# Token-major linear attention with routing inside it, feeding a top-1 mixture of experts: five row tiles per expert and a left-over loop

## The chip, the cores and the metric

The kernel runs on one core of a Trainium2 chip. The metric is the device time of one execution in microseconds (us); the kernel before has a median of 692.61 us over three runs. The engines are TensorE (PE, with its weight loads PEld), VectorE (DVE), ScalarE (ACT), GpSimd (POOL) and the queue engine SyncE (SP). DMAs are issued from the SP queue and from POOL's.

## What is computed

```python
kv  = np.einsum('bhsd,bhse->bhde', k, v)          # q, k, v: 8 x 8 heads x 576 x 64, f32
out = np.einsum('bhsd,bhde->bhse', q, kv)
rms = np.sqrt(np.mean(out * out, axis=-1, keepdims=True) + 1e-06)
x   = (out / rms * g_norm) -> rows of 8 heads * 64 = 512, N = 4608 tokens
logits = x @ w_gate                               # 512 x 8
expert_idx = argmax(logits); gate_w = softmax(logits)[expert_idx]
for e in range(8):                                # w1: 512 x 1024, w2: 1024 x 512
    out[mask_e] = gate_w[mask_e] * (relu(x[mask_e] @ w1[e]) @ w2[e])
```

With the inputs of this kernel the eight experts get 564, 494, 600, 572, 539, 654, 585 and 600 tokens.

## The kernel before

The work stands in three stages, one after the other.

**Attention** (L131 to L215) runs over 8 batches and 4 pairs of heads. It works feature-major: q is turned by PE transposes (`qtp`, L151) and copied by DVE (`qts`, L157), k and v give `kvf` (L161, five f32 matmuls of 128x128 for a pair of heads, of which only the two diagonal 64x64 blocks are copied out), and `otp` (L174, L175) is 128 features by 576 tokens. ACT squares it, a matmul with `sel` (L182) sums the squares over the features, ACT takes Ln and Exp (L185, L187), and DVE multiplies into `roll` (L189) and casts into `xp01`/`xp23` (L198). The logits of each 128 tokens are four f32 matmuls with 8 moving columns (`lgp`, L207). q, k and v come in 256-byte runs on the SP queue (L136 to L142), with two buffers for a batch's `qkv`.

**Routing** (L222 to L325): x is turned back to token rows (L226, L232) and written to the scratch `x16d` (L233); the logits of all tokens give positions by a prefix sum on DVE, and 36 rounds of three DVE operations and one matmul (L299 to L311) turn positions into a list of tokens per slot (`ipv`, `ipu`) and the sorted gates.

**Experts** (L354 to L405): every expert has a capacity `CAP` of 1024 slots, 8 tiles of 128, filled or not. For each expert POOL issues two weight loads that cast to f16 (L349, L351), 8 gathers of rows (L338) and 8 scatters of results (L397). PE does 32 transposes (`xet`, L365), 64 matmuls `hp` of 512 columns (L377) and 64 matmuls `yp` (L390); ACT applies relu (L384), and DVE scales by the gate into `ysb` (L396, 3 buffers). Each scatter writes to the whole of `out`, so it waits for the scatter before it to land.

The order on each engine is set by the framework's scheduler, not by the order in which the code is written; waits between engines, on reused buffers and on overlapping DRAM writes are put in by the framework.

## Time and profile before

| | us |
|---|---|
| median of 3 runs | 692.61 (690.14 to 693.09) |
| span of the profiled execution | 691.4 |
| attention, from the first matmul to the last logits | 10 to 302 |
| routing tables and the scratch of x | 302 to 344 |
| first weights and gathers, start of the first expert | 344 to 374 |
| experts | 374 to 680 |
| last scatters and the end | 680 to 691.4 |

The median lies 1.2 us above the span. In the page, the clock line (PEclk) gives TensorE's granted clock in tenths of full speed, so 1.00 in a window is 2.4 GHz and 0.50 is 1.2 GHz; the DMA line is the busy share of the 16 DMA engines. A line of the trace with f32 matmuls counts two instructions for one matmul of the program, except for transposes, which count one.

### The profile page before, as it was taken

What the parts mean: (1) busy time and instruction counts of PE and PEld (TensorE: products, weight loads), DVE (VectorE), ACT (ScalarE), POOL (GpSimd) and SP (SyncE); (2) the same over time, 40 slices, a digit from 0 to 9 for tenths busy, and PEclk for the clock granted to TensorE, in tenths of its full rate; (3) what the DMA queues carried; (4) which work ended last, traced back from release to release, by engine and by line L of the source; (5) the groups of instructions that cost most, each with busy time, mean ns of one, the idle gap of its engine ahead of it and who ended that gap; (6) DMA issues with size and microseconds to landing.
All of it is one profiled execution on the core that took longest, in us unless ns stands there. A gap on an engine that the chain in (4) does not pass through costs nothing. (4 is left out here: it accounts for less than half of the span.)

```text
span 691.4 us, 6499 instructions
## 1 busy us (share of the span) xinstructions
PE 525.5 (76%) x2458; PEld 321.5 (46%) x2458; DVE 228.1 (33%) x569; ACT 145.6 (21%) x226; POOL 139.4 (20%) x148
## 2 busy tenths in 40 slices
PE   2688787879797879677809569698887959699890
PEld 1547575747474747465604234243433424244440
DVE  0142625252525252569901131212213121222220
ACT  0021313141313131300005005050321305031310
POOL 0000000000000000000055436162544526222222
PEclk9999957586657675757858979998999999999996
DMA  8969191928282900013289726455554626541010
GB/s 144 209 100 182 37 169 35 171 49 157 49 158 51 154 0 1 0 67 134 76 174 186 140 64 128 104 111 118 118 106 100 124 77 119 110 93 46 25 46 26
DMA packets 140302, 68.40 MB, mean 99 GB/s; under 512 B 118639, under 2 KB 131823, under 8 KB 140272
## 3 DMA queue, kind: packets, MB, share of 16 engines
q1 hardware_dynamic: 119536, 33.38, 26.1%
q0 software_dynamic: 20736, 34.63, 24.4%
q8 instruction: 19, 0.31, 0.2%
q14 instruction: 11, 0.09, 0.0%
HBM read 70.59 MB, written 21.50 MB: 133 GB/s over the span
## 5 line engine op out<-in xcount | busy, mean ns | idle before, releaser
L390 PE MATMUL yp<-w2e,hT 128*128 128x512 f16 x512 | 125.0, 402 | 41.5 <-DVE ysb L396 41.4
L384 ACT ACTIVATE hT<-hp 128x512 f16<-128x512 f32 x128 | 76.4, 597 | 278.6 <-PE hp L377 278.6
L396 DVE TENSOR_SCALAR ysb<-yp,gsort 128x512 f32<-128x512 f32 x64 | 48.0, 751 | 239.1 <-DMA out_dram<-ysb,ipu 108.2
L377 PE MATMUL hp<-xsE,w1e 128*128 128x512 f16 x512 | 117.5, 386 | 0.0
L390 PEld LDWEIGHTS <-hT 128*128 128x128 f16 x512 | 52.1, 102 | 112.6 <-issue 59.7
L397 POOL DMA_INDIRECT out_dram<-ysb,ipu x64 | 63.2, 987 | 174.8 <-DMA out_dram<-ysb,ipu 75.3
L161 PE MATMUL kvf<-qkv 128*128 128x128 f32 (+1 forms) x320 | 72.8, 389 | 9.1 <-DMA qkv<-in_v_dram 9.1
L349 POOL DMA_DIRECT2D w1e<-in_moe_w_dram x8 | 7.0, 870 | 346.8 <-DVE ipv L324 346.8
L377 PEld LDWEIGHTS <-w1e 128*128 128x128 f16 x512 | 50.3, 99 | 56.8 <-issue 1.8
L207 PE MATMUL lgp<-wgt,roll 128*128 128x8 f32 x288 | 62.0, 342 | 12.9 <-DVE roll L189 12.9
L161 PEld LDWEIGHTS kvf<-qkv 128*128 128x128 f32 (+1 forms) x320 | 61.3, 277 | 16.5 <-issue 9.2
L207 PEld LDWEIGHTS lgp<-wgt,roll 128*128 128x128 f32 x288 | 60.2, 307 | 16.8 <-DVE roll L189 16.2
L338 POOL DMA_INDIRECT xe<-x_scratch,ipv x64 | 61.5, 961 | 26.5 <-issue 11.9
L180 ACT ACTIVATE sq<-ots 128x576 f16<-128x576 f32 x32 | 21.8, 682 | 196.4 <-DVE ots L177 196.4
L174 PE MATMUL otp<-qts,kv 128*128 128x512 f32 x64 | 50.9, 888 | 12.8 <-DVE qts L157 10.9
L365 PE MATMUL xet<-ident,xe 128*128 128x128 f16 x256 | 25.2, 236 | 28.8 <-issue 16.1
L157 DVE COPY qts<-qtp 128x576 f32<-128x576 f32 x32 | 24.2, 758 | 68.5 <-PE qtp L151 68.2
L151 PE MATMUL qtp<-ident,qkv 128*128 128x128 f32 (+1 forms) x160 | 37.0, 349 | 9.8 <-DMA qkv<-in_q_dram 9.8
L365 PEld LDWEIGHTS <-xe 128*128 128x128 f16 x256 | 19.7, 106 | 39.3 <-issue 34.8
L182 PE MATMUL msp<-sq,sel 128*128 128x512 f16 x32 | 15.4, 483 | 25.6 <-ACT sq L180 24.0
L151 PEld LDWEIGHTS qtp<-ident,qkv 128*128 128x128 f32 (+1 forms) x160 | 23.9, 178 | 23.0 <-issue 20.4
L189 DVE SCALAR_TENSOR_TENSOR roll<-ots,g,rst 128x576 f32<-128x576 f32 x32 | 26.1, 816 | 23.4 <-ACT rst L187 22.5
(61 smaller groups left out, 325.0 us busy)
## 6 DMA issues: line engine op xcount, KB each, us to landing
qkv<-in_q_dram SPq DMA_DIRECT2D x32, 256.0 KB, 4.9
qkv<-in_k_dram SPq DMA_DIRECT2D x32, 256.0 KB, 5.1
qkv<-in_v_dram SPq DMA_DIRECT2D x32, 256.0 KB, 5.2
w1e<-in_moe_w_dram POOLq DMA_DIRECT2D x8, 1024.0 KB, 8.7
w2e<-in_moe_w_dram POOLq DMA_DIRECT2D x8, 1024.0 KB, 9.2
x_scratch<-xtk SPq DMA_DIRECT2D x36, 128.0 KB, 1.7
qkv<-in_q_dram SPq DMA_DIRECT2D x8, 128.0 KB, 5.0
qkv<-in_k_dram SPq DMA_DIRECT2D x8, 128.0 KB, 4.5
```

The source lines that it names most:

```text
L151: nc.tensor.transpose(qtp[:, c * 128 : c * 128 + L], qkv[:L, c, 0, h0 : h0 + 2, :], ident[:L, :L],)
L161: nc.tensor.matmul(kvf, qkv[:L, c, 1, h0 : h0 + 2, :], qkv[:L, c, 2, h0 : h0 + 2, :], start=(c == 0), stop=(c == 4),)
L174: nc.tensor.matmul(otp[:, 0:512], kv2, qts[:, 0:512], start=True, stop=True)
L189: nc.vector.scalar_tensor_tensor(out=roll[:, i, rcol : rcol + 576], in0=ots, scalar=g2, in1=rst, op0=ALU.mult, op1=ALU.mult,)
L207: nc.tensor.matmul(lgp, roll[:, i, lc : lc + 128], wgt[:, i, :], start=(i == 0), stop=(i == 3),)
L338: nc.gpsimd.indirect_dma_start(out=xe, out_offset=None, in_=x16d.ap(), in_offset=IndirectOffsetOnAxis(ap=ipv[:, g : g + 1], axis=0),)
L365: nc.tensor.transpose(xet[:, cset, :], xcur[gg][:, cset * 128 : (cset + 1) * 128], ident16,)
L377: nc.tensor.matmul(hp, w1e[:, kk, f * 128 : (f + 1) * 128], xsE[:, kk, ws * 512 : ws * 512 + 512], start=(kk == 0), stop=(kk == 3),)
L384: nc.scalar.activation(hT[:, f, ws * 512 : ws * 512 + 512], hp, ACTF.Relu)
L390: nc.tensor.matmul(yp, hT[:, ft, cg * 128 : (cg + 1) * 128], w2e[:, ft, :], start=(ft == 0), stop=(ft == 7),)
L396: nc.vector.tensor_scalar(ysb, yp, gsort[:, g : g + 1], None, op0=ALU.mult)
L397: nc.gpsimd.indirect_dma_start(out=out, out_offset=IndirectOffsetOnAxis(ap=ipu[:, g : g + 1], axis=0), in_=ysb, in_offset=None, bounds_che ...
```

## The change

The kernel is written anew. Attention is token-major: `x_tile` handles 128 tokens at a time for all 8 heads (36 tiles), with the turned q stationary and `kvs` moving. `kvs` has 144 columns for a pair of heads: the 128 of kv, and 16 with kv times the gate weights (`kgp`), so the logits fall out of the same matmul. The sums over features are a DVE reduction along the row. `kv_stage` computes only the 64x64 blocks. g_norm moves into `gw` and into w1, which POOL now multiplies and casts after a plain f32 load.

`route` runs after every 4 or 5 tiles: it ranks the tokens within their expert by matmuls with triangular and all-ones matrices, puts token number and gate into the last 4 halfwords of each row, and POOL scatters the rows of 1032 bytes straight to `xs`, which has room for all tokens in each expert. `dram_disjoint_views` tells the framework that the scatters into `xs` and into `out` don't overlap. The weights of six experts are loaded during attention into six buffers.

Each expert has 5 tiles of 128 slots (CAP 640); `left_over` handles what is above, one tile always and more in a loop whose count comes from the data. With these inputs only expert 5 is over 640, by 14 tokens, so the one tile is used and the loop is not entered.

```diff
-    CAP = 1024
+    CT = 5
+    CAP = CT * 128
...
+    xs_views = dram_disjoint_views(xs.ap(), N // 128)
+    out_views = dram_disjoint_views(out, E * CT + 2)
...
+    def load_w(e, stage):
+        e = e if isinstance(e, bass.DynSlice) else slice(e, e + 1)
+        w1e = P_w.tile([128, 4, F], F16, tag="w1e", bufs=6, name="w1e")
+        w2e = P_w.tile([128, 8, D], F16, tag="w2e", bufs=6, name="w2e")
+        for kk in range(4):
+            st = stage.tile([128, F], F32, tag="wst", bufs=2, name="wst")
+            nc.gpsimd.dma_start(
+                st, moe_w1[e, kk * 128:(kk + 1) * 128, :].rearrange("o p f -> p (o f)")
+            )
+            nc.gpsimd.tensor_scalar(
+                w1e[:, kk, :], st, g2, 1.0, op0=ALU.mult, op1=ALU.mult
+            )
+        nc.gpsimd.dma_start(
+            w2e, moe_w2[e, :, :].rearrange("o (t p) d -> p (o t) d", p=128)
+        )
+        return w1e, w2e
...
+        def load_qkv(src, b, tag, bufs):
...
+            nc.sync.dma_start(
+                t, src[b, :, 0:512, :].rearrange("h (p j) d -> p h (j d)", j=4)
+            )
...
+        def load_q(b):
...
+            for j in range(4):
+                nc.sync.dma_start(t[:, j, :, :], qv[:, :, j, :])
...
+        def kv_stage(b, kb, vb, kr, vr):
...
+            for i in range(4):
+                for j in range(5):
+                    for hh in range(2):
...
+                        if j < 4:
+                            lhs = kb[:, h, 64 * j:64 * j + 64]
...
+                        nc.tensor.matmul(
+                            kvp[64 * hh:64 * hh + 64, i, :], lhs, rhs,
+                            start=(j == 0), stop=(j == 4),
+                        )
...
+            for hh in range(2):
+                ps = slice(64 * hh, 64 * hh + 64)
+                nc.vector.tensor_copy(kvs[ps, :, 64 * hh:64 * hh + 64], kvp[ps, :, :])
+            kvtp = PSA.tile([128, 4, 128], F32, tag="misc", bufs=1, name="kvtp")
+            for i in range(4):
+                nc.tensor.transpose(kvtp[:, i, :], kvs[:, i, 0:128], ident)
+            kvt = PA.tile([128, 4, 128], F32, tag="kvt", bufs=1, name="kvt")
+            nc.scalar.copy(kvt, kvtp)
...
+            for i in range(4):
+                nc.tensor.matmul(
+                    kgp[:, i, :], kvt[:, i, :], gw[:, i, :, :], start=True, stop=True
+                )
+            nc.vector.tensor_copy(kvs[:, :, 128:144], kgp)
+            return kvs
+        def x_tile(qsrc, parts, xg, lr, t):
...
+            for i in range(4):
+                nc.tensor.transpose(qtp[:, i, :], qsrc(i), ident)
+            qts = PA.tile([128, 4, 128], F32, tag="qts", bufs=2, name="qts")
+            nc.scalar.copy(qts, qtp)
+            op = PSA.tile([128, 2, 512], F32, tag="op", bufs=2, name="op")
+            for i in range(4):
+                c0 = (i % 2) * 144
+                for c, kvs in parts:
+                    nc.tensor.matmul(
+                        op[c, i // 2, c0:c0 + 144],
+                        qts[:, i, c],
+                        kvs[:, i, :],
+                        start=True,
+                        stop=True,
                     )
...
+            nc.scalar.activation(
+                sq.rearrange("p (c i h) n -> p c i (h n)", c=2, i=2),
+                oc[:, :, :, 0:128], ACTF.Square,
+            )
...
+            nc.vector.reduce_sum(ms, sq, axis=AXX)
...
+            nc.scalar.activation(lnt, ms, ACTF.Ln, scale=1.0 / 64.0, bias=epsb)
...
+            nc.scalar.activation(rinv, lnt, ACTF.Exp, scale=-0.5)
...
+            nc.vector.tensor_tensor(
+                xg[:, t, 0:512].rearrange("p (c i h n) -> p c i h n", c=2, i=2, h=2),
+                ox,
+                _bc(r4, 4, 64),
+                op=ALU.mult,
+            )
+            nc.vector.tensor_tensor(
+                lr[:, t, :, :].rearrange("p (c i h) n -> p c i h n", c=2, i=2),
+                ol,
+                _bc(r4, 4, 8),
+                op=ALU.mult,
+            )
...
+        def route(G, xg, lr, tile0):
...
+            nc.tensor.matmul(pp, ones, _bc(cs16, 1, G), start=True, stop=False)
+            for t in range(G - 1):
+                nc.tensor.matmul(
+                    pp[:, t + 1:G, :], ones, _bc(oh[:, t, :], 1, G - 1 - t),
+                    start=False, stop=False,
+                )
+            nc.tensor.matmul(pp, utri, oh, start=False, stop=True)
...
+            for t in range(G):
+                nc.gpsimd.indirect_dma_start(
+                    out=xs_views[tile0 + t],
+                    out_offset=IndirectOffsetOnAxis(ap=sli[:, t:t + 1], axis=0),
+                    in_=xg[:, t, :].bitcast(I32),
+                    in_offset=None,
+                )
+        for P in range(4):
...
+            kb = load_qkv(k, b0, "kb", 1)
+            vb = load_qkv(v, b0, "vb", 1)
...
+            qb0 = load_q(b0)
+            qr = load_rem(q, b0, "qr", 2)
+            kvs0 = kv_stage(b0, kb, vb, kr, vr)
...
+            for j in range(4):
+                x_tile(
+                    lambda i: qb0[:, j, 2 * i:2 * i + 2, :],
+                    [(slice(0, 128), kvs0)], xg, lr, j,
+                )
...
+            route(4, xg, lr, 9 * P)
+            kvs1 = kv_stage(b0 + 1, kb, vb, kr, vr)
+            if P < 3:
+                weights[2 * P] = load_w(2 * P, P_w)
...
+        def ffn(xe, nt, w, okm, bgm, views):
...
+            cols = nt * 128
+            halves = 2 if cols > 512 else 1
+            wd = cols // halves
...
+            for ws in range(halves):
+                for f in range(8):
...
+                nc.gpsimd.indirect_dma_start(
+                    out=views[t],
+                    out_offset=IndirectOffsetOnAxis(ap=idx[:, t:t + 1], axis=0),
...
+        def left_over(t, t0, view):
...
+            w = load_w(bass.ds(ev, 1), P_w)
...
+            ffn([gather(xe_bufs[t0], gi)], 1, w, okm, bgm, [view])
...
+        xcur = load_x(0)
+        for e in range(E):
+            xnext = load_x(e + 1) if e + 1 < E else None
+            if e + 6 < E:
+                weights[e + 6] = load_w(e + 6, P_w)
+            ffn(xcur, CT, weights[e], valid[:, e, :], bigm[:, e, :],
+                out_views[e * CT:(e + 1) * CT])
+            xcur = xnext
+        left_over(0, 2 * CT, out_views[E * CT])
+        nov = nc.values_load(tabi[0:1, 1, 7:8], min_val=0, max_val=NOV)
+        with tc.If(nov > 1):
+            with tc.For_i(1, nov) as t:
+                left_over(t, 2 * CT + 1, out_views[E * CT + 1])
```

Three places show what the scheduler makes of it. The first is PE inside attention. Before, in the middle of a batch (`otp` is the product with kv, `msp` the sum of squares, `lgp` the logits):

```order
L174 MATMUL otp<-qts,kv_339 128x512
L175 MATMUL otp<-qts,kv_339 128x64
L207 MATMUL lgp<-wgt,roll 128x8
L182 LDWEIGHTS sel
L182 MATMUL msp<-sq,sel 128x512
L183 LDWEIGHTS sel
L183 MATMUL msp<-sq,sel 128x64
L151 MATMUL qtp<-ident,qkv 128x128 x4
L151 MATMUL qtp<-ident,qkv 128x64
```

Now, at the end of the third pair's first batch (`op` is the product with kv and the logits, `pp` the ranks in `route`, `kvp` the next batch's kv):

```order
L218 MATMUL op<-kvs_94,qts 128x144 x8
L211 MATMUL qtp<-cf,qb 128x128 x8
L285 LDWEIGHTS ch
L285 MATMUL pp<-cs_1233,ch 128x32
L218 MATMUL op<-kvs_94,qts 128x144 x8
L287 LDWEIGHTS ch
L287 MATMUL pp<-oh,ch 128x24
...
L291 LDWEIGHTS ch
L291 MATMUL pp<-oh,ch 128x32
L186 MATMUL kvp<-vb,kb 64x64 x8
```

The rank matmuls, which need the result of the last two tiles (`oh`), stand in PE's queue ahead of the next batch's `kvp`. The second place is POOL's queue. Before, it holds nothing but a branch ahead of the first weight load and the gathers behind it:

```order
L349 DMA w1e_2113<-in_moe_w_dram 128x4x1024 [waits DMAHW3_49,DMAHW2_49,DMAHW4_49,DMAHW1_49,DMAHW5_49,DMAHW0_49,DMAHW6_49,DVE_49,DMAHW7_49,PE_49,Activation_49]
L351 DMA w2e_2115<-in_moe_w_dram 128x8x512
L338 DMA xe_2117<-x_scratch,ipv 128x512
L338 DMA xe_2119<-x_scratch,ipv 128x512
L338 DMA xe_2121<-x_scratch,ipv 128x512
```

Now it holds during attention (here the end of the first pair's first batch and the beginning of its second):

```order
L131 TENSOR_SCALAR w1e<-wst,g_65 128x1024 [waits DMASW4_49]
L131 TENSOR_SCALAR w1e<-wst,g_65 128x1024 [waits DMASW5_49]
L304 DMA xs_scratch<-xg,sli 36864x258 [waits DVE_49]
L304 DMA xs_scratch<-xg,sli 36864x258 x2
L304 DMA xs_scratch<-xg,sli 36864x258 [waits DMASW2_49]
L128 DMA wst<-in_moe_w_dram 128x1024 [waits DMASW3_49,Pool_49]
L128 DMA wst<-in_moe_w_dram 128x1024 [waits Pool_49]
L134 DMA w2e<-in_moe_w_dram 128x8x512
```

Weight loads and casts now stand between the row scatters in one queue: 10 of the 24 w1 pieces and all six w2 loads are issued ahead of the second batch's scatters. The third place is POOL in the experts' stage. Before, in expert 0:

```order
L397 DMA out_dram<-ysb,ipu 4608x512 [waits DMASW5_49,DVE_49]
L397 DMA out_dram<-ysb,ipu 4608x512 [waits DMASW6_49,DMASW5_49,DVE_49]
L397 DMA out_dram<-ysb,ipu 4608x512 [waits DMASW7_49,DMASW6_49,DVE_49]
L397 DMA out_dram<-ysb,ipu 4608x512 [waits DMASW7_49,DMASW0_49,DVE_49]
L397 DMA out_dram<-ysb,ipu 4608x512 [waits DMASW1_49,DMASW0_49,DVE_49]
```

Now, in a late expert:

```order
L476 DMA out_dram<-ys,idx 4608x512 [waits DMASW6_49,DVE_49]
L502 DMA xe_82<-xs_scratch,rowi 128x258 [waits DMASW7_49,PE_49]
L476 DMA out_dram<-ys,idx 4608x512 [waits DMASW0_49,DVE_49]
L502 DMA xe_83<-xs_scratch,rowi 128x258 [waits DMASW1_49,PE_49]
L476 DMA out_dram<-ys,idx 4608x512 [waits DMASW2_49,DVE_49]
```

Before, a scatter waits for the semaphore of the scatter just ahead of it (DMASW5, then 6, 7, 0); now it waits only for the semaphore that was used eight POOL DMAs earlier and for its data.

## Rows read from the trace of the kernel before

**Rows 1.** The page: span, granted clock and DMA share in 40 slices.
```profile
span 691.4 us, 6499 instructions
...
PEclk9999957586657675757858979998999999999996
DMA  8969191928282900013289726455554626541010
```
**Rows 2.** Stretches: start:end, length, busy of PE, PEld, DVE, ACT, POOL, PEclk, DMA share, GB/s.
```profile
10.00:302.00 292.00, 231.49 (x960) 175.06 (x959) 113.86 (x258) 67.42 (x96) 0.00 (x0) 0.74 0.56 96
302.00:344.00 42.00, 32.74 (x213) 24.29 (x214) 40.33 (x172) 0.44 (x1) 0.00 (x0) 0.74 0.32 113
344.00:374.00 30.00, 13.44 (x73) 7.95 (x73) 5.03 (x19) 4.46 (x8) 18.16 (x19) 0.61 0.92 162
374.00:680.00 306.00, 247.65 (x1215) 114.00 (x1213) 68.22 (x120) 71.98 (x121) 118.09 (x122) 0.94 0.46 98
```
**Rows 3.** Waits, by total: engine and line, whom for: us, times, longest.
```profile
POOL w1e L349 <- DVE ipv L324: 346.8, 1, 346.8
...
DVE ysb L396 <- DMA out_dram<-ysb,ipu: 108.2, 36, 11.9
...
PE yp L390 <- DVE ysb L396: 41.4, 16, 10.0
```
**Rows 4.** Timeline of PE in attention: start us, us, engine, line, operation, count.
```profile
12.22 1.20 PE L161 MATMUL kvf<-qkv 128*128 128x128 f32 x4 [1.97 <-DMA qkv<-in_v_dram]
...
62.14 4.50 PE L161 MATMUL kvf<-qkv 128*128 128x128 f32 x18
...
72.06 0.84 PE L151 MATMUL qtp<-ident,qkv 128*128 128x128 f32 x5
...
79.67 0.56 PE L207 MATMUL lgp<-wgt,roll 128*128 128x8 f32 x4
...
89.82 6.14 PE L207 MATMUL lgp<-wgt,roll 128*128 128x8 f32 x28 [1.49 <-DVE roll L189]
...
102.43 2.39 PE L161 MATMUL kvf<-qkv 128*128 128x128 f32 x16
...
115.79 1.39 PE L151 MATMUL qtp<-ident,qkv 128*128 128x128 f32 x5
```
**Rows 5.** Groups by line: shapes, count | busy us, mean ns | idle before.
```profile
L189 DVE SCALAR_TENSOR_TENSOR roll<-ots,g,rst 128x576 f32<-128x576 f32 x32 | 26.1, 816 | 23.4 <-ACT rst L187 22.5
...
L157 DVE COPY qts<-qtp 128x576 f32<-128x576 f32 x32 | 24.2, 758 | 68.5 <-PE qtp L151 68.2
...
L180 ACT ACTIVATE sq<-ots 128x576 f16<-128x576 f32 x32 | 21.8, 682 | 196.4 <-DVE ots L177 196.4
...
L274 DVE SCALAR_TENSOR_TENSOR pos<-ix,ss 128x36 f32<-128x36 f32 x1 | 0.2, 196 | 0.0
```
**Rows 6.** Two stretches by the columns of rows 2: early attention, one expert.
```profile
20.00:60.00 40.00, 31.21 (x103) 21.75 (x102) 13.86 (x31) 8.44 (x12) 0.00 (x0) 1.00 1.06 163
...
411.00:448.00 37.00, 31.96 (x159) 14.53 (x157) 7.62 (x14) 9.56 (x16) 16.76 (x18) 0.95 0.56 116
```
**Rows 7.** POOL's indirect DMAs: a group by line, and issues with us to landing.
```profile
L338 POOL DMA_INDIRECT xe<-x_scratch,ipv x64 | 61.5, 961 | 26.5 <-issue 11.9 <-DMA w2e<-in_moe_w_dram 7.4 <-PE hp L377 5.8
...
xe<-x_scratch,ipv POOLq DMA_INDIRECT x64, 4.4
out_dram<-ysb,ipu POOLq DMA_INDIRECT x64, 2.7
```
**Rows 8.** Timeline of the experts' stage, by the columns of rows 4.
```profile
447.61 0.61 PE L365 MATMUL xet<-ident,xe 128*128 128x128 f16 x8
...
452.75 12.90 PE L377 MATMUL hp<-xsE,w1e 128*128 128x512 f16 x59
...
659.84 12.25 PE L390 MATMUL yp<-w2e,hT 128*128 128x512 f16 x56
...
687.66 0.97 POOL L397 DMA_INDIRECT out_dram<-ysb,ipu  x1 [1.87 <-DMA out_dram<-ysb,ipu]
```

More of the change, by code (lines that the diff above doesn't have):

```diff
@@ L127 @@
+    weights = {}
     with (
@@ L202 @@
-            while (next_w + 1) * 128 <= (b + 1) * 576:
-                w = next_w
-                lc = 128 * (w % 9)
-                lgp = PSA.tile([128, 8], F32, tag="KV", bufs=2)
-                for i in range(4):
-                    nc.tensor.matmul(
-                        lgp,
-                        roll[:, i, lc : lc + 128],
-                        wgt[:, i, :],
-                        start=(i == 0),
-                        stop=(i == 3),
-                    )
-                nc.vector.tensor_copy(logits[:, w, :], lgp)
-                next_w += 1
@@ new lines @@
+        cs16 = PA.tile([128, 8], F16, tag="cs16", bufs=2, name="cs16")
+        nc.vector.tensor_copy(cs16, csum)
+        cp = PSA.tile([128, 8], F32, tag="misc", bufs=1, name="cp")
+        nc.tensor.matmul(cp, ones, cs16, start=True, stop=True)
+        cnt = PA.tile([128, 8], F32, tag="cnt")
+        nc.vector.tensor_copy(cnt, cp)
+        nc.vector.tensor_tensor(valid, _bc(rankc, 1, E), _bc(cnt, 2, CT), op=ALU.is_lt)
+        nc.vector.tensor_scalar(
+            bigm, valid, -BIG, BIG, op0=ALU.mult, op1=ALU.add
+        )
@@ new lines, in gather, with load_x @@
+        def gather(xe, rows):
+            nc.gpsimd.indirect_dma_start(
+                out=xe.bitcast(I32),
+                out_offset=None,
+                in_=xs.ap(),
+                in_offset=IndirectOffsetOnAxis(ap=rows, axis=0),
+                bounds_check=E * N - 1,
+                oob_is_err=False,
+            )
+            return xe
+        def load_x(e):
+            return [
+                gather(xe_bufs[(e % 2) * CT + t], rowi[:, e, t:t + 1])
+                for t in range(CT)
+            ]
```

511 lines of the change are left out of this document (240 added, 271 removed).

## The prediction

> **What bounds the kernel now.** I read the page's slices first, then the stretches, then the waits, and only then single rows. The slices show a clock near half speed and a DMA share that comes in bursts up to slice 16, a DMA pause, and a clock near full speed from slice 23 [rows 1]. The stretches say where the 691.4 us go: 292 us of attention with PE busy for 231 of them at a mean granted clock of 0.74, 42 us in which DVE is busy for 40.3 (routing), 30 us in which PE does 13 us of work and the DMA share is 0.92, and 306 us of experts with PE busy for 248 at 0.94 [rows 2]. So PE bounds attention and the experts, DVE the routing, and the first loads the start of the experts. The waits show what is loose: POOL issues no weight load before 346.8 us, since that waits for the routing; and in the experts PE waits 41.4 us for DVE, which waits 108.2 us for the previous scatters to land [rows 3]. The sum below is made against the span; the median is 1.2 us above it.
>
> **Attention, 292 us to some 252.** The prices on PE first, for a matmul of the program (two lines in f32, one for a transpose). A 128x128 kv matmul takes 2.39/8 = 0.30 us where the clock is at 2.4 GHz and 4.50/9 = 0.50 at 1.2 GHz; a transpose 0.17 and 0.28; a logits matmul with 8 columns 0.28 and 0.44 [rows 4]. That eight columns cost nearly as much as 128 says that the f32 weight load sets the pace.
> The 144 logits matmuls, `msp`, the casts to `xp` and the turning back go. What comes, for a pair of batches:
> - kv: 80 matmuls of 64x64. No row has that shape. Half the weight columns bound it below by half the 128x128 price (0.15 and 0.25), above by all of it (0.30 and 0.50). I take 0.18 and 0.28, near the lower end, as the weight load sets the pace and is halved: 14.4 and 22.4 us.
> - transposes: 36 of q and 8 of kv, 44 x 0.17 or 0.28 = 7.4 or 12.2.
> - `op`: 36 matmuls, 4 more for the tile that two batches share, at the 128x128 price (144 columns under the same weight load): 12 or 20.
> - `kgp`: 8 at the logits price, 2.2 or 3.5. The eleven rank matmuls: 1 or 2.
> PE thus has 37 us of work at the upper clock and 60 at the lower. Then its waits. From kv to the first `op` PE waits for two DVE copies, ACT's copy of `kvt` and DVE's copy of `kgp`: 2 x 3 us beyond the transposes that fill part of it. A tile's chain is Square 0.68, reduction 0.7, Ln and Exp on 8 columns 0.4 together, two products 0.82 + 0.2, all by the nearest shapes [rows 5], 3.2 us with handovers; with two `op` buffers and 1.9 us of PE work this sets 2.6 us a tile at the upper clock and adds 6 us a pair, and nothing at the lower, where PE needs 3.1. Once a pair the rank matmuls wait in PE's queue ahead of `kvp` for the chain and some seven small DVE steps of 0.2 [rows 5]: 6 us. So a pair takes 37 + 6 + 6 + 6 = 55 at the upper clock, 60 + 6 + 6 = 72 at the lower. Before, the mean clock lay about midway at 0.74, and PE's share of the time will be like it (0.75 against 231/292); I take 58.
> DMA next. q stays in 256-byte runs, and so do the last 64 rows of k and v: by the shapes 11.5 MB, at 163 GB/s for a share of 1.06 [rows 6], 75 us. k and v in runs of 1 KB: 16.8 MB; x's scratch writes, also 1 KB, moved 113 GB/s at a share of 0.32 [rows 2], or 353 at a full share, so 48 us. Row scatters: 4.75 MB, 14 us. An expert's weights: the 37 us of one expert are 0.56 busy, 20.7 us, less 1.05 MB gathered and 1.18 MB scattered at 353, leaves 14.4; six make 86. Together 223 us of a full share in some 250: it fits, with little room. Ten w1 pieces and all of w2 fall into the first pair: 58 us beside its own 32, so I add 8 us there. The start stays at 12 us, as now [rows 4]: 2.6 MB come before the first product is complete. 12 + 4 x 58 + 8 = 252.
> By the Trainium skill, "DMA: Bandwidth & Descriptors", section "Issuing engines are not separate DMA queues", DMAs from different engines run on the same 16 DMA engines and interleave. It speaks against loading weights in attention for free, and the share of 1.06 [rows 6] agrees that q, k and v alone can fill them; by it, the high rival below.
>
> **POOL's casts, nothing on the path.** 24 casts of 128x1024 stand between the row scatters. No row has POOL computing on a wide tile; DVE's 128x576 takes 0.76 to 0.82 [rows 5], so 1.4 us by length, and I take 2.5 as POOL should be the slower. 24 x 2.5 + 36 scatters x 1.26 + some 46 other issues and fills x 1 = 150 us, under the 252. Below 0 it can't go; if the cover fails, it is the slow rival.
> The Trainium skill, "GPSIMD Engine Reference", section "Performance versus the Vector engine", calls GpSimd the wrong engine for elementwise work and has 4497 ns for a two-input add of 2048 f32, 1.96 times VectorE; a cast at half of it is an estimate of 2.25 us, and the sum would be the same. No run so far shows it.
>
> **Routing and the start of the experts, 72 us to some 25.** The 42 us of routing tables go, and the weights are already there. What stays exposed is a chain behind the last `op`: tile chain and 18 small DVE steps with a PE trip, 10 us; five scatters at 0.96 + 0.3 us issue each on POOL, and 2.7 to land, 9 us; five gathers at the same spacing, with 2.7 to land at the least and 4.4 at the median [rows 7], 8 us to the last tile's transpose. 27, less the 2.8 counted at each expert's beginning: 24, I say 25. The left-over tables (some 20 DVE steps) run beside the scatters; without that cover they cost 4 us more.
>
> **Experts, 306 us plus the tail of 11.4 to 175.** `hp` runs at 12.90/59 = 0.219 us for 512 columns, so 0.137 for 320, as the weight load is not the limit: eight transposes with a load each take 0.61 us, 0.076 apiece. `yp` stays at 12.25/56 = 0.219 [rows 8]. An expert: 64 x 0.137 + 40 x 0.219 = 17.5; between `yp` and the next `hp`, DVE's last scaling and three copies, 2.8. 20.3 x 8 = 162. The scatter chain goes: a scatter no longer waits for the one ahead, and five in 20 us even at the chained 3.7 us each (0.97 + 2.7) would fit. What is late next: POOL, with 10 indirect DMAs x 1.26 = 12.6 us an expert; not the end. The left-over tile: copy and scaling 1.7, 32 x 0.076, relu 1, 8 x 0.219, scaling 1: 8 us. From the last scatter to the end 3.7, as now, from 687.66 to 691.4 [rows 1, 8]; for loading the loop count and branching on every engine 1.5, between 0 and 6. 175 in all.
>
> **Sum.** 252 + 25 + 175 = 452, plus 1.2: 453 us.
>
> **Rivals.**
> Low: the kv matmuls, alternating between the two halves of the output, overlap, and the clock stays up: 0.12 for each gives 50 us a pair; no collision in the first pair. 12 + 200 + 25 + 175 + 1 = 413. For it: the weight load sets the pace. Against: a clock of 0.74 under a like PE share.
> High: attention at the lower clock, or held by the DMA engines: 72 us a pair and the 8: 12 + 296 + 25 + 175 + 1 = 509. For it: 223 us of DMA work, and single buffers for k and v, so that their load can't start before the last kv product of the batch ahead. Against: PE's work between two kv stages (some 20 us) covers 9 us of loading.
> POOL's indirect DMAs go one by one: if each took 3.7 us until landed, because waits for semaphores eight DMAs back bunch, an expert takes 37 us, as now, and the total is 453 + 8 x 16.7 = 587. Then the new views don't do what they say. Against: gathers issue 1.26 us apart today [rows 7].
> Slower than before: POOL's casts hold up the row scatters, which stand behind them in the queue, and so the end of attention. POOL has 90 us of other work; over 489 us of attention, where 692 is reached, each of the 24 casts would need (489 - 90)/24 = 16.6 us, twelve times DVE's price by length. At 20 us: 480 + 90 + 10 to start + 25 + 175 = 780. For it: no row prices POOL. Against: the factor.
>
> **How the numbers follow.** Forecast 0.52 (430 to 480), low 0.18, high 0.23, POOL one by one 0.04, casts 0.03. The range reaches from the low rival to a little beyond the high one, 408 to 515, and leaves out some 0.12, with the edges of the low rival. A change within 0.5%, about what a measurement can tell from none, would need one of the bad cases to fall just there: 0.01. Slower 0.03, faster 0.96.
>
> **What would show it.** Right: attention ends near 252 us with a clock of 0.65 to 0.8; between the last `op` and the first `hp` some 27 us; an expert every 20 us with no DVE wait for `out`. Wrong: PE waiting for `kb` or `vb` (DMA), `kvp` at 0.3 us or more, POOL casts above 4 us, DVE waiting for a scatter in the experts, or more than 10 us after the last `yp`.

## The result, and the profile after

The changed kernel takes 458.21 us at the median (453.91 to 459.49, 4 runs) against 692.85 for the kernel before (690.14 to 694.30, 4 runs): a ratio of 0.661, 95% interval 0.657 to 0.665. The prediction was 453 us in a range of 408 to 515. The total is right, but of its four parts two are far off and cancel, so that it came this close is luck.

| stage, by the profiled execution (span 457.6 us) | predicted | measured | difference |
|---|---|---|---|
| start to the end of the last `op` | 252 | 232.5 | -19.5 |
| to the transposes of expert 0 | 25 | 20.8 | -4.2 |
| eight experts, to the end of the last one's `yp` (442.0) | 162 | 188.7 | +26.7 |
| left-over tile and end | 13 | 15.6 | +2.6 |
| span | 452 | 457.6 | +5.6 |

(Expert 0's first `hp` starts at 256.1; 2.8 us for its transposes, as the prediction counted them, are taken off the second row and added to the third.)

The page of the changed kernel, span, granted clock and DMA share in 40 slices of 11.4 us, beside [rows 1]:

```profile
span 457.6 us, 6059 instructions
...
PEclk9999787557597757976765699979879998989996
DMA  8999789999599979991002237667464221222020
```

The DMA engines, which had a pause in the middle of the kernel before, are now at nine tenths or more in 13 of the 18 slices up to 206 us, and loose after. The four pairs of batches begin (first `kvp`) at 10.3, 73.8, 134.2 and 183.3 us. By the columns of [rows 2] (start:end, length, busy of PE, PEld, DVE, ACT, POOL, clock, DMA share, GB/s):

```profile
10.00:73.00 63.00, 35.55 (x290) 30.70 (x290) 17.50 (x51) 14.29 (x36) 18.44 (x21) 0.92 1.04 233
73.00:134.00 61.00, 35.33 (x311) 31.45 (x311) 19.97 (x60) 13.64 (x35) 24.16 (x27) 0.64 1.02 257
134.00:183.00 49.00, 35.11 (x312) 31.60 (x312) 22.77 (x65) 15.27 (x41) 24.89 (x29) 0.72 1.03 284
183.00:233.00 50.00, 35.62 (x330) 31.26 (x329) 23.64 (x71) 17.68 (x47) 8.69 (x9) 0.79 0.50 122
```

PE has the same 35 us of work in each pair, the DMA share is above 1 in three of them, and the first two are 11 to 14 us longer than the others. What PE waits for there (us in total, times, longest; one of the seven waits of `pp`, 4.8 us, is behind the last `op`):

```profile
PE pp L287 <- DVE oh L269: 30.7, 7, 5.9
PE qtp L211 <- DMA qb<-in_q_dram: 17.6, 4, 5.8
PE kvp L186 <- DMA vb<-in_v_dram: 14.1, 2, 10.3
PE op L218 <- DVE lr L246: 13.3, 9, 2.2
PE kvp L186 <- DMA vr<-in_v_dram: 10.8, 2, 9.5
```

In the experts' stage the 108.2 us in which DVE waited for scatters [rows 3] are gone but for 6.4, and the gathers have taken their place:

```profile
DVE ys L473 <- PE yp L468: 69.2, 29, 10.0
DVE idx L445 <- DMA xe<-xs_scratch,rowi: 60.1, 29, 10.4
DVE ys L473 <- DMA out_dram<-ys,idx: 6.4, 1, 6.4
```

From one expert's first `hp` to the next one's it takes 21.4, 25.7, 30.2, 24.3, 22.1, 23.3, 21.3 and 18.7 us, where the prediction had 20.3. The end of expert 2, the longest, by the timeline (POOL, DVE and PE; start us, us, what, idle before and who ended it):

```profile
318.68 2.28 POOL L131 TENSOR_SCALAR w1e<-wst,g 128x1024 f16<-128x1024 f32 x2 [4.28 <-DMA wst<-in_moe_w_dram]
319.34 0.75 DVE L473 TENSOR_SCALAR ys<-yp,xe 128x512 f32<-128x512 f32 x1 [0.98 <-PE yp L468]
...
321.79 1.06 POOL L476 DMA_INDIRECT out_dram<-ys,idx  x1 [0.31 <-issue]
...
323.15 1.06 POOL L502 DMA_INDIRECT xe<-xs_scratch,rowi  x1 [0.30 <-issue]
...
326.14 1.91 DVE L445 SCALAR_TENSOR_TENSOR idx<-xe,valid,bigm 128x1 int32<-128x1 int32 x1 [6.04 <-DMA xe<-xs_scratch,rowi]
...
327.98 0.74 DVE L473 TENSOR_SCALAR ys<-yp,xe 128x512 f32<-128x512 f32 x1
...
329.47 0.74 DVE L441 COPY xt<-xp 128x512 f16<-128x512 f16 x2
...
329.93 1.01 PE L438 MATMUL xp<-ch,xe 128*128 128x128 f16 x8 [6.73 <-DVE xt L441]
```

POOL waits 4.3 us for a weight load, so the scatter and the gather behind it in its queue come late. DVE's `idx` is the row number of a tile that expert 4 will need; it waits for that gather with the fourth `ys` of expert 2 and the `xt` of expert 3 behind it. PE loses 6.7 us for a number that is due two experts later.

The granted clock has a part too. The `hp` products of an expert take 8.7 us at the upper clock, as in expert 1, and 10.9 in expert 3 (by the same columns, PE alone):

```profile
277.60:286.30 8.70, 8.70 (x68) 1.00 0.93 170
333.50:344.40 10.90, 10.90 (x66) 0.79 0.72 137
```

PE does not stop in either. In the second the clock is at the lower level up to 338.0 us; it had fallen at 327.8, while PE stood waiting for DVE.

For three of the experiments (e1, e13, e20) the profiled execution was 1.5 to 2.2% longer than the shortest timed one, so that their profiles are read for which waits there are and their sizes below are that much too long; the ratios leave such executions out, the medians don't.

### The profile page after: what moved, and what is told of

It is laid out like the page before. It is cut to its first block, busy times and chain, and to the rows that moved or that the text cites. A ratio compares the mean times of both kernels' runs of the same rounds, so it can differ in the third digit from the quotient of the medians.

```text
span 457.6 us, 6059 instructions
## 1 busy us (share of the span) xinstructions
PE 308.5 (67%) x2281; PEld 224.6 (49%) x2281; DVE 149.4 (33%) x418; ACT 121.0 (26%) x297; POOL 195.7 (43%) x220
## 5 line engine op out<-in xcount | busy, mean ns | idle before, releaser
L462 ACT ACTIVATE ht<-hp 128x320 f16<-128x320 f32 (+1 forms) x136 | 57.9, 428 | 150.8 <-PE hp L455 139.7
L455 PE MATMUL hp<-xt,w1e 128*128 128x320 f16 (+1 forms) x544 | 81.7, 315 | 0.9 <-DVE xt L441 0.9
L304 POOL DMA_INDIRECT xs_scratch<-xg,sli x36 | 35.5, 986 | 95.6 <-DVE sli L302 63.4
L468 PE MATMUL yp<-w2e,ht 128*128 128x512 f16 x328 | 72.4, 379 | 0.0
L476 POOL DMA_INDIRECT out_dram<-ys,idx x41 | 41.3, 1009 | 68.4 <-DVE ys L473 62.5
L131 POOL TENSOR_SCALAR w1e<-wst,g 128x1024 f16<-128x1024 f32 x36 | 40.2, 1119 | 70.6 <-DMA wst<-in_moe_w_dram 57.4
L455 PEld LDWEIGHTS <-w1e 128*128 128x128 f16 x544 | 55.4, 105 | 25.3 <-issue 1.1
L218 PE MATMUL op<-kvs,qts 128*128 128x144 f32 (+1 forms) x320 | 51.5, 337 | 17.5 <-DVE lr L246 13.3
L218 PEld LDWEIGHTS op<-kvs,qts 128*128 128x128 f32 (+1 forms) x320 | 46.4, 219 | 21.1 <-ACT rinv L238 8.8
L468 PEld LDWEIGHTS <-ht 128*128 128x128 f16 x328 | 32.1, 98 | 37.3 <-issue 0.3
L502 POOL DMA_INDIRECT xe<-xs_scratch,rowi x40 | 40.9, 1023 | 14.5 <-issue 10.1
L438 PE MATMUL xp<-ch,xe 128*128 128x128 f16 x164 | 16.6, 244 | 41.5 <-DVE xt L441 26.1
L186 PEld LDWEIGHTS kvp<-vb,kb 128*64 128x64 f32 x512 | 26.4, 198 | 17.3 <-issue 10.2
L211 PEld LDWEIGHTS qtp<-cf,qb 128*128 128x128 f32 x128 | 23.8, 208 | 19.6 <-DMA qb<-in_q_dram 15.4
L445 DVE SCALAR_TENSOR_TENSOR idx<-xe,valid,bigm 128x1 int32<-128x1 int32 x40 | 10.9, 273 | 66.5 <-DMA xe<-xs_scratch,rowi 65.6
```

Source lines behind the costliest of these rows:

```text
L131: nc.gpsimd.tensor_scalar(w1e[:, kk, :], st, g2, 1.0, op0=ALU.mult, op1=ALU.mult)
L186: nc.tensor.matmul(kvp[64 * hh:64 * hh + 64, i, :], lhs, rhs, start=(j == 0), stop=(j == 4),)
L211: nc.tensor.transpose(qtp[:, i, :], qsrc(i), ident)
L218: nc.tensor.matmul(op[c, i // 2, c0:c0 + 144], qts[:, i, c], kvs[:, i, :], start=True, stop=True,)
L304: nc.gpsimd.indirect_dma_start(out=xs_views[tile0 + t], out_offset=IndirectOffsetOnAxis(ap=sli[:, t:t + 1], axis=0), in_=xg[:, t, :].bitca ...
L438: nc.tensor.transpose(xp[:, c, :], xe[t][:, c * 128:(c + 1) * 128], ident16)
```

## The experiments

Twelve runs, each timed in rounds beside the kernel before (medians 690.2 to 691.4 us there). "Attention" is the end of the last `op`, "experts" from the first `hp` to the end of the last `yp`, the left-over's included, both in the profiled execution. The last two columns divide the eight experts: "`hp`" is the sum of their times from the first `hp` to the first `yp` (8.7 us each, 69.6 in all, where nothing disturbs them), "changes" the sum of the seven times from the last `yp` of one expert to the first `hp` of the next, where the prediction had 2.8 each, 19.6 in all. The `yp` products take 70.4 to 70.9 us for eight experts in every run but e20 (77.5).

| run | median us | ratio to before | attention | experts | `hp` | changes |
|---|---|---|---|---|---|---|
| changed kernel | 458.2 | 0.661 | 232.5 | 190.9 | 78.2 | 37.0 |
| e1 no loads among the experts | 465.6 | 0.668 | 237.3 | 198.3 | 93.5 | 29.3 |
| e2 casting transfer | 462.1 | 0.671 | 232.1 | 192.7 | 86.4 | 30.9 |
| e3 idx per tile | 470.6 | 0.681 | 230.7 | 201.7 | 86.0 | 40.3 |
| e5 half of the weight loads in attention | 446.3 | 0.646 | 212.4 | 195.9 | 87.6 | 32.9 |
| e13 idx tied | 463.5 | 0.668 | 235.5 | 193.9 | 92.5 | 25.7 |
| e4 kv on one half | 493.3 | 0.712 | 261.1 | 197.7 | 85.9 | 36.2 |
| e6 two k, v buffers | 459.5 | 0.666 | 221.7 | 199.6 | 87.3 | 36.4 |
| e14 four edits | 415.8 | 0.602 | 197.6 | 187.4 | 84.0 | 27.6 |
| e19 tied, ten ys | 457.2 | 0.663 | 236.5 | 183.0 | 87.6 | 19.7 |
| e20 ten ys | 470.3 | 0.678 | 239.4 | 199.1 | 85.0 | 31.5 |
| e18 four edits, ten ys | 416.1 | 0.602 | 197.9 | 189.4 | 93.1 | 20.5 |
| e21 late weights | 395.2 | 0.571 | 177.8 | 184.9 | 89.9 | 19.1 |

### What makes the kv products so cheap: e4

```diff
-                for j in range(5):
-                    for hh in range(2):
+                for hh in range(2):
+                    for j in range(5):
                         h = 2 * i + hh
```

> The 40 kv products of a batch are issued five in a row on one half of the columns, then five on the other, where the changed kernel alternates between the halves; same products, same number. In the changed kernel one costs 0.146 us at the lower clock and 0.087 at the upper, far under the 0.28 of the prediction's sum. Theory F (two products on different halves run beside each other): the price goes to 0.2 or more at the lower clock, 320 products cost 15 to 25 us more on PE, of which the waits for q, k and v hide a part: 464 to 480 us. Rival G (a product costs this little by itself, for its 64 columns): the price stays within 0.02 us and the time within 4 us of the changed kernel.

493.3 us. The timeline of the changed kernel, at the lower and the upper clock (one product is two records):

```profile
163.68 1.12 PE L186 MATMUL kvp<-vb,kb 128*64 128x64 f32 x16
164.74 0.48 PE L186 MATMUL kvp<-vr,kr 64*64 64x64 f32 x4
165.15 1.12 PE L186 MATMUL kvp<-vb,kb 128*64 128x64 f32 x16
...
186.96 0.69 PE L186 MATMUL kvp<-vb,kb 128*64 128x64 f32 x16
187.57 0.33 PE L186 MATMUL kvp<-vr,kr 64*64 64x64 f32 x4
187.84 0.69 PE L186 MATMUL kvp<-vb,kb 128*64 128x64 f32 x16
```

and of e4, at the same two clocks:

```profile
52.02 1.12 PE L186 MATMUL kvp<-vb,kb 128*64 128x64 f32 x8
53.07 0.47 PE L186 MATMUL kvp<-vr,kr 64*64 64x64 f32 x2
53.47 1.11 PE L186 MATMUL kvp<-vb,kb 128*64 128x64 f32 x8
...
151.59 0.68 PE L186 MATMUL kvp<-vb,kb 128*64 128x64 f32 x8
152.20 0.33 PE L186 MATMUL kvp<-vr,kr 64*64 64x64 f32 x2
152.45 0.68 PE L186 MATMUL kvp<-vb,kb 128*64 128x64 f32 x8
```

From the start of one group to the next, the changed kernel issues ten products in 1.47 us (0.147 each) and 0.88 (0.088); e4 five in 1.45 (0.290) and 0.86 (0.172). About the same time takes twice the products when they alternate, as theory F has it: two products on different halves of the columns run beside each other. No run tests a second reading, that products which add into the same output wait for one another, but a row of the changed kernel speaks against it. Eight `op` products, which add into nothing, cost 0.275 us each at the upper clock, about as much as the 0.30 of the kv products before, which do add [rows 4]:

```profile
181.14 2.20 PE L218 MATMUL op<-kvs,qts 128*128 128x144 f32 x16 [1.57 <-DVE lr L246]
```

320 products cost 320 x 0.14 = 46 us more at the lower clock and 27 at the upper; attention ends 28.6 us later. The total is above the 464 to 480 expected, since the experts' stage, which the edit does not touch, took 6.8 us longer as well. The prediction's prices, 0.18 and 0.28, are those of products that do not overlap.

### What sets the pace of attention: e5 and e6

e5 (experts 1 to 5 multiply with expert 0's tiles):

```diff
-                weights[2 * P] = load_w(2 * P, P_w)
+                weights[2 * P] = load_w(0, P_w) if P == 0 else weights[0]
...
-                weights[2 * P + 1] = load_w(2 * P + 1, P_w)
+                weights[2 * P + 1] = weights[0]
```

> Leaves out five of the six weight loads of the attention stage: experts 1 to 5 multiply with expert 0's tiles, so 20 MB less are read by 200 us. In the changed kernel the pairs begin at 10.3, 73.8, 134.2 and 183.3 us, and the last operation ends at 232.5. Theory D (the DMA engines are full up to 200 us, and the first two pairs wait for q, k and v behind the weights' bytes): the first two pairs fall from 63.5 and 60.4 to about 50 us, attention ends at 205 to 212, and the kernel takes 430 to 438 us. Rival E (one buffer each for k and v: a load starts when the last kv product has read the buffer, and PE waits for that transfer whatever else runs): the pairs lose less than 4 us each, 450 to 458 us.

The edit leaves out less in attention than was meant. With five buffers free, the scheduler brings the loads of experts 6 and 7 forward from the experts' stage: three sets are issued during attention (12 of the 24 `w1` pieces, three of the six `w2`), not one, and only the left-over's load stays behind.

e6 (the loads of both batches, and the sums' buffers; the small tiles `ms`, `lnt` and `t1` lose a buffer each too):

```diff
-            kb = load_qkv(k, b0, "kb", 1)
-            vb = load_qkv(v, b0, "vb", 1)
+            kb = load_qkv(k, b0, "kb", 2)
+            vb = load_qkv(v, b0, "vb", 2)
...
-            kvs = kvs_bufs[b % 4]
+            kvs = kvs_bufs[b % 2]
```

> Two buffers each for k and v instead of one, so that a batch's k and v are read while the one before is in use (two buffers for the kv sums instead of four make room). Without five of the weights the attention stage ended 20 us earlier, which says that bytes hold it. Theory D (the DMA engines are full): only the stretches with a share under 1 can be filled, 0.79 in 40 to 60, 0.91 in 100 to 120, 0.86 in 160 to 180 us, together 9 us: attention ends at 222 to 229 instead of 232.5, the kernel takes 447 to 456 us. Rival E (the wait for the one buffer holds PE): the pairs come to 50 us as the last two have it, attention ends at 207 to 215, 433 to 441 us.

e5 ends attention at 212.4 us, 20 earlier; e6 at 221.7, 11 earlier. The first pair of e5 issues the same loads as the changed kernel up to 58 us and takes 64 us as before; its second falls from 60 to 46. By the columns above, the second pair of e5:

```profile
74.00:120.00 46.00, 35.86 (x310) 31.39 (x311) 18.38 (x60) 13.63 (x35) 16.87 (x19) 0.68 0.97 235
```

and the first three pairs of e6, where two buffers only bring a DMA share of 1.12 to 1.13 and the first pair is 68 us:

```profile
10.00:78.00 68.00, 39.52 (x287) 34.36 (x288) 14.66 (x45) 12.18 (x30) 18.18 (x21) 0.85 1.13 241
78.00:128.00 50.00, 33.74 (x315) 29.63 (x314) 20.85 (x65) 15.40 (x41) 23.34 (x26) 0.76 1.13 291
128.00:173.00 45.00, 32.41 (x322) 28.68 (x322) 22.93 (x66) 15.89 (x43) 19.32 (x24) 0.81 1.12 296
```

Both agree with theory D for the stage: the bytes of the weights hold q, k and v up, and a second buffer fills what was idle. Since e5 spared half of the loads and not five sixths, 20 us is the price of three sets. The rule that the prediction weighed, from the Trainium skill, "DMA: Bandwidth & Descriptors", "Issuing engines are not separate DMA queues", is borne out: loads on POOL's queue came out of the time of those on SP's. The totals fell short (446.3 against 430 to 438; 459.5 against 447 to 456), since the experts took 5 and 9 us longer. In e6 code and order of that stage are those of the changed kernel on every engine, and the table says where the 9 us are: `hp` takes 87.3 us instead of 78.2, the changes are the same. Why is taken up with e19.

### What holds the experts: e1, e2, e3, e13, e20, e19

Six runs, for three candidates: POOL's queue (A), the loads' bytes (B), DVE's wait for gathers (C).

```diff
-                weights[e + 6] = load_w(e + 6, P_w)
+                weights[e + 6] = weights[e]
...
-            w = load_w(bass.ds(ev, 1), P_w)
+            w = weights[5]
```

> Leaves out the weight loads of the experts' stage: experts 6 and 7 multiply with the tiles of experts 0 and 1, the left-over tile with those of expert 5. In the changed kernel experts 1, 2 and 3 take 25.7, 30.2 and 24.3 us from first hp to first hp, where the prediction had 20.3 each: 19 us too much, in the stretch in which POOL's queue holds the loads and casts of these weights. Theory A (the queue: a cast that waits for its load holds the row scatters and gathers behind it) and theory B (the bytes of the loads slow the gathers and scatters down) both give about 458 - 19 = 439 us, with 20 to 22 us for each of the eight experts. Theory C (DVE waits for the next expert's gathers, in the idx computation, ahead of the scaling that frees PE) has no part in these loads: 455 us or more.

e2 (and the same for the left-over):

```diff
+        nc.gpsimd.dma_start(
+            w1e, moe_w1[e, :, :].rearrange("o (t p) f -> p (o t) f", p=128)
+        )
...
+        for kk in range(4):
+            nc.scalar.mul(w1e[:, kk, :], w1e[:, kk, :], g2)
...
-                weights[e + 6] = load_w(e + 6, P_w)
+                weights[e + 6] = load_w_cast(e + 6)
```

> The weights w1 of experts 6, 7 and the left-over come by one transfer each that casts to f16 on the way, and ACT multiplies them by g in place; the same bytes are read, and POOL waits for no load. Theory A (POOL's queue): the 19 us of experts 1 to 3 go as they do without the loads, less up to 4 us for ACT's twelve products of 128x1024 among the relus: 438 to 444 us. Theory B (bytes): no gain, 455 to 460 us, and experts 1 to 3 still take 24 to 30 us. Theory C: no gain either.

e3 (the five `idx` of line 445 go):

```diff
+                idx = PF.tile([128, 1], I32, tag=f"idx{nt}", bufs=4, name="idx")
+                nc.vector.scalar_tensor_tensor(
+                    out=idx, in0=xe[t][:, 512:514].bitcast(I32),
+                    scalar=okm[:, t:t + 1], in1=bgm[:, t:t + 1],
...
                 ys = PF.tile([128, D], F32, tag="ys", bufs=4, name="ys")
```

> The scatter's row numbers (idx) are written one tile at a time, beside the scaling of that tile, and no longer five at once behind the transposes; POOL's queue is as it was. Theory C (DVE's wait for the next expert's gathers, 65.6 us in 40 idx instructions, stands ahead of xt and ys on DVE): experts 1 to 7 get 1 to 3 us shorter each, 440 to 450 us. Theories A and B: the gathers come when POOL issues them, PE then waits for them at its transposes instead; within 3 us of the changed kernel, 455 to 461 us.

None gained: 465.6, 462.1, 470.6 us. Without any load, no expert of e1 stands out any more, and all but the last are long, 24 to 26 us. DVE still waits for the gathers, oftener and shorter:

```profile
DVE idx L445 <- DMA xe<-xs_scratch,rowi: 54.2, 39, 3.0
```

So A and B are not enough. But the totals hide a part of A: the changes behind experts 1 and 2, 8.1 and 10.7 us in the changed kernel, are 4.6 and 4.9 in e1 and 4.9 each in e2, where the same bytes are read and POOL waits for no load. What was won there was lost again in longer `hp` phases (93.5 and 86.4 us in the table).

e3 did not test C: the scheduler again placed `idx` tiles of the next expert ahead of `ys` and `xt`. With four buffers, they now wait for earlier scatters, for as long as the old ones did for gathers:

```profile
DVE idx L466 <- DMA out_dram<-ys,idx: 60.1, 31, 7.7
```

In e13 `idx` can't stand there, since it reads a number made from the tile's own `yp`:

```diff
+                bgy = PF.tile([128, 1], F32, tag="bgy", bufs=4, name="bgy")
+                nc.vector.tensor_scalar(
+                    bgy, yp[:, 0:1], 0.0, bgm[:, t:t + 1], op0=ALU.mult, op1=ALU.add
+                )
...
+                    scalar=okm[:, t:t + 1], in1=bgy,
```

> The kernels of the first four runs keep DVE's idx of the next expert but one, which waits for a row gather that POOL has only just issued, ahead of ys and xt in DVE's queue. Here idx of a tile also reads a number that is made from that tile's own yp, so that it can stand nowhere ahead of the expert's own ys. Everything else is as in the changed kernel. Theory C (DVE's wait for gathers not yet needed): the experts' periods, 21.4 to 30.2 us, come down to 20 to 21.5 each, 187 us for eight become about 166, and the kernel takes 435 to 441 us. Rival A (POOL's queue: loads and casts of later weights between scatters and gathers): experts 1 to 3 keep 24 to 30 us and only the later ones lose some 2 us each: 446 to 453 us.

463.5 us, and a miss for both. The changes fall from 37.0 to 25.7 us and `hp` rises from 78.2 to 92.5. No `idx` waits for a gather any more, but in three experts the fifth `ys` waits for one of four buffers, that is for the first scatter, which POOL issued late behind a cast:

```profile
DVE ys L476 <- DMA out_dram<-ys,idx: 6.0, 3, 3.1
```

e20 gives `ys` ten buffers in the changed kernel, e19 in e13 (`idx` and `bgy` too):

```diff
-                ys = PF.tile([128, D], F32, tag="ys", bufs=4, name="ys")
+                ys = PF.tile([128, D], F32, tag="ys", bufs=10, name="ys")
```

> Ten buffers for ys and nothing else changed: DVE's order of instructions is the same as in the changed kernel, and idx still waits for the next gathers ahead of ys and xt. Theory H (either wait alone is enough): little gain, 452 to 461 us. Rival I (the scatters' landings alone held DVE): 435 to 443 us.

> The run with idx tied to its own tile still had experts of 23 to 26 us: DVE's fifth ys of an expert waited for its buffer, one of four, that is for the landing of the expert's first scatter, which POOL had issued late behind casts. Here idx is tied and ys has ten buffers, so that DVE waits neither for a gather nor for a scatter; POOL's queue is as in the changed kernel. Theory H (both waits, each of which alone is enough to hold xt and with it PE): the experts' periods come to 20 to 21.5, the kernel takes 435 to 443 us. Rival A (POOL's queue itself is late with the gathers): PE's transposes wait for rows in experts 2 to 4 instead, 448 to 460 us.

e20 does not gain (470.3, above both expectations): the scatter's buffer alone was not it, and `idx` waits as before, up to 16.0 us in one place. e19, with both waits gone, has experts of 23.4, 20.1, 20.0 and 21.4 us and then 23.8, 26.3 and 25.3. `hp` and `yp` of experts 2 and 5 (start:end, length, busy PE, clock, DMA share, GB/s):

```profile
303.00:312.40 9.40, 9.21 (x73) 1.00 0.53 190
312.40:321.20 8.80, 8.80 (x46) 1.00 1.05 196
...
368.90:376.00 7.10, 3.91 (x24) 0.78 0.27 87
376.00:383.90 7.90, 7.90 (x47) 0.77 0.00 0
383.90:392.70 8.80, 8.80 (x46) 1.00 0.23 76
```

Theory H holds for experts 1 to 3, where POOL's queue is fullest: with neither wait they take 20.0 to 21.4 us, as the prediction had them, and POOL's lateness costs nothing. It holds for the changes as a whole: 19.7 us for seven, where the prediction had 19.6 and the changed kernel 37.0. It fails for the kernel (457.2, not 435 to 443): `hp` took 9.4 us more and attention 4 more than in the changed kernel. The 457.2 lies in the range of rival A, but PE does not wait for rows in experts 2 to 4, as A has it. In experts 5 and 6 PE stops for 3.0 and 3.4 us after its first twelve `hp` products, and its clock is at the lower level for part of what follows:

```profile
373.79 10.25 PE L448 MATMUL hp<-xt,w1e 128*128 128x320 f16 x52 [3.04 <-issue]
```

"issue" is a wait for which this line names nobody. DVE and ACT in the same microseconds, and the waits of e18, which has the same stops, say more:

```profile
370.39 0.42 DVE L441 COPY xt<-xp 128x512 f16<-128x512 f16 x1 [1.72 <-PE hp L448]
373.30 0.44 ACT L455 ACTIVATE ht<-hp 128x320 f16<-128x320 f32 x1 [13.80 <-remote]
...
PE hp L462 <- ACT ht L469: 7.8, 6, 2.9
```

Twelve products fill the three `hp` buffers, and the thirteenth starts as ACT's first relu ends, at 373.7 ("remote": the view names no releaser). But that relu reads products that the trace has as ended at 369.7, and DVE's copy at 370.4 reads transposes that it has as ended at 368.1. Both waited for PE's semaphore, which rose at 370.4, 371.8, 373.2 and 374.6 us, 1.4 apart. In expert 2 it rises 0.54 us apart for four `hp` products each, within 0.02 of the recorded ends. The ends of matmuls are modelled in the profile, so the slow one here is PE itself, already before the stop shows. Why stays open; the DMA share is 0.27, which makes bytes unlikely. Such stops and time at the lower clock are what lengthens `hp` in e4, e6 and e13 too: the stops above 0.3 us come to 3.9, 5.5 and 9.9 us there, and to none in the changed kernel.

### Together: e14, e18, e21

e14 has the tied `idx`, two buffers each for k, v and their remainders, the second batch's kv products ahead of `route(4, ...)`, and four weight buffers:

```diff
-            if P < 3:
+            if P < 2:
...
-            if e + 6 < E:
-                weights[e + 6] = load_w(e + 6, P_w)
+            if e + 4 < E:
+                weights[e + 4] = load_w_cast(e + 4)
```

> Four edits together: idx tied to its own tile as in e13; four weight buffers, of which attention fills four and no longer six, while experts 4 to 7 and the left-over are loaded during the experts, w1 by a casting transfer and multiplied by g on ACT; two buffers each for k, v and their remainders; the second batch's kv products in program order ahead of the first batch's ranks. If theories C and D hold, attention ends at 200 to 212 us (a third of the weights' bytes gone, as in the run with one weight), the transition stays at 24 to 26, the experts take 166 to 172, and the kernel takes 405 to 422 us. If the loads of the experts' stage then hold the gathers up, the experts take 185 or more: 425 to 440 us.

415.8 us, within the 405 to 422 expected, though neither part is as expected: attention ends at 197.6, earlier than the 200 to 212, and the experts take 187.4, not 166 to 172. No run tells the four edits apart; in particular the place of the kv products ahead of `route` was not tried alone. e18 is e14 with ten buffers for `ys` and `idx`:

> The run with four edits together (415.8 us; attention ended at 197.6, the experts took 183 us) with ten buffers for ys and idx. Theory H: the experts come to 20 to 21.5 us each, 166 to 172 in all, 400 to 407 us. Rival J (the loads that are read among the experts hold the row gathers up in the transfers themselves): experts 1 to 4 stay at 22 to 25 us and PE waits for xe: 410 to 417 us.

416.1 us: no gain, as rival J has it by its number, but not by its mechanism, since PE waits for `xe` 17.3 us, 12.2 of them ahead of the first expert. The changes fall from 27.6 to 20.5 us, as theory H has it, and `hp` rises from 84.0 to 93.1, with stops like those of e19 (2.9, 2.8 and 3.4 us after twelve products). Both e14 and e18 spend 64 us in the first pair, in which all four `w2` loads and eight of the 16 `w1` pieces are issued. e21 spreads them:

```diff
+        nc.gpsimd.tensor_copy(w2e[:, 0, 0:1], tie)
...
+            nc.gpsimd.tensor_copy(st[:, 0:1], tie)
...
+            weights[P] = load_w(P, P_w, kvs1[:, 0, 0:1])
```

> As the run before it in this call, and each of the four weight loads of the attention stage starts only when the kv sums of its pair's second batch are there (its buffers take a number from them first), one a pair, where so far all four started as early as buffers let them and the first pair took 64 us, the later ones 41. Theory D (the first pair waits for q, k and v behind the weights' bytes): the first pair falls to 48 to 54 us, attention ends at 180 to 190, 386 to 397 us with experts as in the run before. Rival K (the first pair is held by its own 7 MB, which nothing hides, and the last weights and casts now hold POOL's scatters at the stage's end): attention ends at 193 or later or the transition grows from 23 to 30 us: 402 us or more.

395.2 us, ratio 0.571 (0.568 to 0.573), 0.86 of the changed kernel's median, and the best of all. Its first pair and its last:

```profile
10.00:50.00 40.00, 31.10 (x298) 26.77 (x300) 15.22 (x46) 12.59 (x31) 6.36 (x10) 1.00 1.12 252
...
131.00:178.00 47.00, 32.31 (x327) 28.43 (x324) 23.19 (x70) 16.56 (x46) 20.29 (x29) 0.83 0.81 192
```

Theory D: 39 us for the first pair, less than the 48 to 54 expected, and attention ends at 177.8, earlier than the 180 to 190. Of rival K one half came true in part: from the last `op` to the first `hp` it is 27.3 us instead of e18's 23.6, not the 30 that K named.

## Why the prediction came out right

**The step that failed in the experts** is "20.3 x 8 = 162": the work in it is right, the waits are missing. `hp` and `yp` of the last expert, with nothing in the way:

```profile
424.50:443.10 18.60, 17.68 (x111) 10.41 (x109) 4.54 (x8) 7.00 (x16) 3.97 (x5) 1.00 0.15 58
```

17.7 us busy against 17.5 predicted, and 8.7 + 8.8 from the first `hp` to the last `yp`. "What is late next: POOL ... 12.6 us an expert; not the end" counted POOL's issues and not that they start at the first `ys`, alternate with gathers, and stand behind casts that wait for loads; nor that DVE, in order, would wait for these gathers ahead of the scaling and the copies that PE needs. e19 shows the 20.3 where DVE has no such wait. Of the 27 us, 17 are in the changes between experts (37.0 us where 19.6 were counted), and e13 and e19 show that they are DVE's waits. Some 9 are in `hp` (78.2 instead of 69.6): 17.7 us of it ran at the lower clock, with no stop of PE, and at half the rate half of that is lost, 8.9. The prediction took `hp` at the price of the upper clock throughout. After the first expert the clock falls four times (at 300.5, 327.8, 379.0 and 402.9 us), each time between the last `yp` of one expert and the first `hp` of the next, where PE waits for DVE. In e19, where those waits are gone, it falls three times, and PE's slow stretches take their place; those stay open.

**The term mis-sized in attention** is kv at 0.18 and 0.28: it measured 0.088 and 0.147, below the lower bound, so the low rival's mechanism (the halves overlap) is true. With half of a pair's 80 products at each price that is 40 x 0.092 + 40 x 0.133 = 9 us a pair. PE's work fell to 35 us, and the first two pairs were then held to 63 and 61 us by the DMA engines, the high rival's mechanism, while the last two took 49. The mechanisms of both rivals came true and worked against each other. The 8 us of collision were put into the first pair alone; they were 11 to 14 in each of two, and of the ten `w1` pieces and six `w2` loads counted there, eight and five were issued before the second pair began. The DMA sum of 223 us "fits, with little room": length times share in the four rows above give 65.5 + 62.2 + 50.5 + 25 = 203, with no room in the first three.

**What held as priced.** The wait of the rank products ahead of `kvp`: 6 us a pair predicted, 24 in all; up to the last `op` it measured 25.9 in six waits, 4.3 each and half as often again as counted. The end of attention to the first `hp`: 27 predicted, 23.6 measured, with `sli`'s five scatters 1.3 us apart:

```profile
238.94 1.09 POOL L304 DMA_INDIRECT xs_scratch<-xg,sli  x1 [23.17 <-DVE bigm L375]
...
244.15 0.96 POOL L304 DMA_INDIRECT xs_scratch<-xg,sli  x1 [0.30 <-issue]
```

Scatters no longer wait for one another, so the rival of POOL going one by one fell. So did the rival of slow casts, which needed 16.6 us each (16.7, as its 489 us of attention give 690 and not 692):

```profile
L131 POOL TENSOR_SCALAR w1e<-wst,g 128x1024 f16<-128x1024 f32 x36 | 40.2, 1119 | 70.6 <-DMA wst<-in_moe_w_dram 57.4
```

1.12 us, under the 2.5 taken and the 1.4 by DVE's price. The estimate of 2.25 us from the Trainium skill, "GPSIMD Engine Reference", "Performance versus the Vector engine", is twice the measured one; it was worked out from an operation with two inputs, and the cast has one. Idle time before casts, 57.4 us for loads, was not in the sum, and is what makes POOL late.

**The end**: the last scatter is issued at 448.03, the span ends at 457.6, so 9.6 us where 3.7 and 1.5 were counted. It is not the loop: e14, e18 and e21 have the same loop and 3.9 us. What it is stays open. Of the signs that the prediction named for its being wrong, three appeared, PE's wait for `vb`, a DVE wait for a scatter and over 10 us behind the last `yp` (10.6); each is one of the parts above.

## What to carry to other kernels

An instruction that is not urgent costs most when it stands in an in-order queue ahead of one that is: look for waits on transfers among small index computations, and if a scheduler places them, tie them to data that only comes when they are due. Loads for a later stage are not free in a stage that fills the DMA engines; start them one at a time, where the queue has room. Where several waits hold the same place, each has to be tried with the others gone. And a total can hide a gain: the changes between experts fell from 37.0 to 19.7 us in e19 while the kernel's time stayed, so divide a stage into its phases before an edit is called useless. After each edit, look at what else the scheduler moved (e5).

## What the runs showed that I had not expected

- Two f32 products of 64 columns on different halves of the output run beside each other: 0.147 against 0.290 us at the lower clock, 0.088 against 0.172 at the upper, by the order of two loops alone.
- POOL casts 128x1024 from f32 to f16 in 1.12 us, faster by length than the 128x576 copies of DVE [rows 5].
- The same code of the experts' stage took 191 us in the changed kernel, 198 in e4 and 200 in e6, where only attention differs and every engine has the same order of instructions in this stage. All of it is in `hp` (78.2, 85.9 and 87.3 us). Why is open.
